# Block attention and a split-precision feed-forward on one core: the weight loads and the split-weight stores issued by GpSimd's queue instead of SP's

## The chip, the core and the metric

The kernel runs on one core of a Trainium2 chip. The metric is the device time of one execution in microseconds; the kernel before has a median of 1163.66 us over 3 runs (1163.17 to 1164.16).

## What is computed

Eight batches of eight heads go through causal block attention (sequence 576, head size 64, blocks of 64), and the result goes through a feed-forward layer with a quadratic gate:

```python
scores = scale * np.matmul(q, k.transpose(0, 1, 3, 2))
mask = block_i >= block_j
scores = np.where(mask, scores, -1000000000.0)
attn = np.exp(scores - np.max(scores, axis=-1, keepdims=True))
attn = attn / (np.sum(attn, axis=-1, keepdims=True) + 1e-09)
x = np.matmul(attn, v)            # -> (4608, 512) after the heads are put side by side
h = x @ w_in                      # (4608, 512) @ (512, 2048)
g = np.where(h >= 1, h, np.where(h <= -1, 0.0, (h + 1) ** 2 / 4))
out = g @ w_out                   # (4608, 2048) @ (2048, 512)
```

q, k and v are float32; the two weight matrices arrive as float64, eight bytes an element.

## The kernel before

**Two parts that overlap.** Attention goes pair of heads by pair of heads (32 pairs, `attention_steps`). The feed-forward goes through 9 chunks of 512 tokens (`c`), and in each through 16 slices of 128 hidden columns (`fc`). `ffn_in` (L852) makes one slice of h in PSUM with three products, high and low halves of x and w_in; ACT and DVE make the gate (L861 to L865), ACT rounds it to its high half `gh` (L866) and GpSimd subtracts it to get the low half `gl` (L867); `ffn_out` multiplies both with the slice of w_out (L880), one step later. The slice of w_out, already split into halves, is read back from the scratch tensor `wo_split` in HBM for each chunk (L869). In the trace the first `gl` starts at 82.10 us.

**The weight pieces.** Before the first chunk can run, the float64 weights must become pairs of float32 words. There are 32 pieces of 128 x 512 (16 of w_in, 16 of w_out), made by `convert` from the generator `weight_pieces`. One piece goes like this:

1. A load brings 512 KB into the tile `bits` (L267). `bits` has three slots, and a load may start when the slot's last reader is done.
2. ACT scales the two halves of the words (L272, L273), DVE clips, shifts and merges them (L274, L277, L280).
3. GpSimd adds the two halves (L286).
4. ACT rounds the sum to the high half (L288: into `wih` or into a staging tile `ws`).
5. GpSimd subtracts to get the low half (L290: into `wil` or `ws`).
6. For a piece of w_out, a store sends the staging tile to `wo_split` (L316). A slot of `ws` can be written again when that store has landed.

In the trace the first load is issued at 0.73 us and the last store at 189.40 us; from there on GpSimd does nothing but `gl`.

**What sets the order.** The order on each engine is written out: the table `QUEUES` holds, for each engine, a list of positions packed as text, and the program ties each instruction to the one in front of it in that order. Each engine works its instructions strictly in that order, so whatever waits holds up all that is listed behind it. DMAs are issued by SP in this kernel (one half of the last output store is issued by ACT). SP's list holds, in the first 190 us, the loads of q, k and v for attention (L433, L440, L444), copies of raw q and k (L387), the masks (L252, L253), the copies of the softmax rows (L348), the reads of `wo_split` (L869), and among them the 32 weight loads and the 16 stores.

**Engines in the text.** PE multiplies and transposes: L494 the first transposes of q and k, L559 the scores of the first batches. ACT's L497 and L499 copy the transposed q and k out of PSUM for L559. DVE's L586 takes row maxima, and L862 and L865 belong to the gate.

Of the kernel before, what the change touches and what calls it, by code (L numbers as in the profile page):

```python
# [11 lines left out]
F32 = mybir.dt.float32  # L12
# [4 lines left out]
I32 = mybir.dt.int32  # L17
# [82 lines left out]
        'avr4!9IO_j+jIP<wb9qip9>eBYQ2yV`U)AJZ{=JOfVBe{F1kw'  # L100
    ),
    "Pool": (
        'c-muNzz-O4@EL)S2~4vBAp|giWf|dWnBZ)LYGfHy)r@eG5lM6ufB*nFCIBn'
    ),
    "SP": (
        'c-rk$yKWOv5IuA6t{=OBc%5K7FR)2W6s1T<LrNMXD5#JS5)}oAf)W~<R1`^>NGWM(kWxe;C11cV<TEHy&YZomAO%=yXmUs6-'
        'JQpoIWt%8AV)Tl0)f(kp^1{(phC|KJJf(SeV_4>)`D8n)0V$Qy-Cd#70|(vaK6%C2%{95M@34PTGC!48sEC~zGuz}pNsV7io'
        '1mYV}Ocz(9<Ie%&3FFYF@D<N}h7|=`qPXqYO6~)y15wo>TYfofM1?sseQ$X>|-s;$Fi7(Y?})5IW-1R7TC(WC_e`QtRI=y+?'
        'Y36v}QT2AQUjv$p}W8@Nw|oLpmyZs4gp@ts7m^xs*$vRV2oieV(gh!;d?<2knZm5EJG&xl`lRP_fLbQK%W({@Z8eU8<nVtvN'
        '=rmlT2OG1Ba{`JU~uqzDT*(c(Rg-|KG(tiDHt9}p1v^tw-d@kxfZ1SzIm`Kj^*w6%lA?;^rIv_*fCl0iyJv){C0p41ReM2}~'  # L110
        'X)_P)mpS4~YtTBfQcQf)-?b&vzM$QiZrMINSx?M^>N>M!L>rp(@8bhqJuxz@D$X&VSV*zJ7kh0BM7&21cQwbDrgdmO*#T$mI'
        'b-S?F#_IMR7_B<Hx4Q;ZQ*B}a%Aob-v_junm_%<AFCI?KXaP!ZLBaKX)70}-dmP#JQ(|@xP2%AZ^Pd*`<LW$W^<BhX^WVm_O'
        'j$EU0*%(n(sB=|I7E{-~L|_0l%LN)17JK>T?cm8a4?'
    ),
}

# [7 lines left out]
def block_attn_then_ffn(  # L124
# [9 lines left out]
    nc = tc.nc  # L134
    B, H, S, D = q.shape
# [43 lines left out]
    def slot(pool, shape, dtype, tag, name):  # L179
        return pool.tile(shape, dtype, tag=tag + next(turns[tag]), name=name)  # L180
# [14 lines left out]
    xl = const.tile([P, NCC, RING], F32R, tag="xl", name="xl")  # L195
# [4 lines left out]
    wo_split = dram.tile([NFC, P, 2, DM], F32, tag="wo_split", name="wo_split")  # L200
# [57 lines left out]
    def wide_tile(dtype, name):  # L258
        return slot(conv, [P, 2 * CW], dtype, "bits", name)

    def convert(n, source, hi, lo, done):

        bits = wide_tile(I32, "bits").rearrange("p (n t) -> p n t", t=2)
        if not shifted:
            shifted.append(att1.tile([P, CW], U32, tag="x32", name="shifted"))
        tmp = shifted[0]
        nc.sync.dma_start(bits, source.bitcast(I32).rearrange("p (n t) -> p n t", t=2))  # L267
        top, low = bits[:, :, 1].bitcast(F32), bits[:, :, 0]
        words = top.bitcast(U32)


        nc.scalar.mul(top, top, 2.0**-112)  # L272
        nc.scalar.mul(low, low.bitcast(U32), 2.0**-29)  # L273
        nc.vector.tensor_scalar(  # L274
            out=top, in0=top, scalar1=F32_TOP, scalar2=-F32_TOP, op0=ALU.min, op1=ALU.max
        )
        nc.vector.tensor_scalar(  # L277
            out=tmp, in0=words, scalar1=3, scalar2=None, op0=ALU.logical_shift_left
        )
        nc.vector.scalar_tensor_tensor(  # L280
            out=words, in0=words, scalar=0x80000000, in1=tmp,
            op0=ALU.bitwise_and, op1=ALU.bitwise_or,
        )
        yield
        w32 = bits[:, :, 1]
        nc.gpsimd.tensor_tensor(out=w32, in0=w32, in1=low, op=ALU.add)  # L286
        w32 = w32.bitcast(F32)
        nc.scalar.copy(hi(), w32)  # L288
        yield
        nc.gpsimd.tensor_tensor(out=lo(), in0=w32, in1=hi().bitcast(F32), op=ALU.subtract)  # L290
        if done:
            done()

    def weight_pieces():

        for f0 in range(0, DF, CW):
            fs = slice(f0, f0 + CW)
            for cc in range(NCC):
                yield (
                    w_in[cc * P : (cc + 1) * P, fs],  # L300
                    lambda cc=cc, fs=fs: wih[:, cc, fs], lambda cc=cc, fs=fs: wil[:, cc, fs], None,
                )
            for fc in range(f0 // P, (f0 + CW) // P):
                ws = {}

                def part(w, d0, ws=ws):
                    if not ws:
                        ws[0] = slot(ffn, [P, 2, DM], F32R, "wo", "ws")
                    return ws[0][:, w, d0 : d0 + CW]

                for d0 in range(0, DM, CW):
                    yield (
                        w_out[fc * P : (fc + 1) * P, d0 : d0 + CW],
                        lambda p_=part, d0=d0: p_(0, d0), lambda p_=part, d0=d0: p_(1, d0),
                        None if d0 + CW < DM else
                        lambda fc=fc, ws=ws: nc.sync.dma_start(wo_split[fc], ws[0].bitcast(F32)),  # L316
                    )

    def prepare_weights():

        live = []
        for n, piece in enumerate(weight_pieces()):
            live = [c for c in live + [convert(n, *piece)] if next(c, True) is None]
            yield
        for _ in range(LAG):
            live = [c for c in live if next(c, True) is None]
            yield
# [662 lines left out]
```

## Time and profile before

| | |
|---|---|
| median of 3 runs | 1163.66 us |
| the profiled execution's own time | 1161.97 us |
| span of the profile in it | 1159.9 us |
| PE busy with matmuls | 1136.7 us (98%) |
| DVE, ACT, GpSimd busy | 700.3, 614.2, 267.7 us |
| weight loads (L267) | 32, 512 KB each |
| stores of split weights (L316) | 16, 512 KB each |

The profile is one execution. "Busy" is time in which an instruction of the engine ran; issuing a DMA is not counted as busy. In rows of the timeline the columns are the start and the duration in us, the engine (SPq is SP's queue issuing a DMA, PEld is PE's weight load), line and operation, output<-input; in square brackets stand the idle time of the engine just before it and what ended that idle time. In rows of groups "x32" is a count.

### The profile page before, as it was taken

The page shows a single profiled execution, that of the slowest core. Times are in us where ns is not written, and L with a number is a line of the kernel's source. Part 1 is how long each engine was busy: PE and PEld are TensorE (multiplying, and loading weights), DVE is VectorE, ACT ScalarE, POOL GpSimd, SP SyncE. Part 2 cuts the span into 40 slices and gives each one's busy share as a digit, 9 for nine tenths or more (in the row PEclk, how much of TensorE's full clock was granted, in tenths as well). Part 3 has the DMA queues.
Part 4 walks back from the last instruction along what each step waited for, and adds up shares of the span by engine and source line. Part 5 has one row for each costly group of instructions (what it writes and reads, how often), then busy time and mean ns, then how long its engine had stood idle before and what let it go on. Part 6 is the DMA issues. An engine that isn't in the chain of part 4 may idle for free.

```text
span 1159.9 us, 19449 instructions
## 1 busy us (share of the span) xinstructions
PE 1136.7 (98%) x6544; PEld 906.6 (78%) x6544; DVE 700.3 (60%) x1731; ACT 614.2 (53%) x1515; POOL 267.7 (23%) x215
## 2 busy tenths in 40 slices
PE   6899999999999999999999999999999999999998
PEld 4667677888887878888888888888888887888886
DVE  7887695766667666666666666666666663222222
ACT  7996675555555555555555555555555553222222
POOL 4445563111111111111111111111111111222222
PEclk9999999999999999999999999999999999999999
DMA  8888787887787866656556555655666443323323
GB/s 227 244 251 264 241 263 228 242 244 221 252 239 245 238 195 181 206 172 188 177 165 214 171 164 176 216 171 167 189 201 177 150 139 110 116 96 105 127 91 108
DMA packets 195793, 219.55 MB, mean 189 GB/s; under 512 B 131296, under 2 KB 145888, under 8 KB 194928
## 3 DMA queue, kind: packets, MB, share of 16 engines
q1 hardware_dynamic: 195552, 218.20, 62.0%
q8 instruction: 52, 0.85, 0.3%
q14 instruction: 45, 0.37, 0.1%
q10 hardware_dynamic: 144, 0.13, 0.0%
HBM read 135.79 MB, written 31.98 MB: 145 GB/s over the span
## 4 chain that ended last, share of the span: by engine, by line
PE 89%; DVE 4%; ACT 2%; DMA 2%; issue 1%; POOL 1%; SPq 0%; POOLq 0%; ACTq 0%
PE ph L852 33%; PE po L880 33%; PE ps_av L730 7%; PE ps_t L651 4%; PE ps_s L535 4%; PE ps_s L536 3%; PE ps_qk L473 1%; PE ps_s L618 1%; ACT pr L591 1%; PE ps_s L559 1%; DMA bits<-in_moe_w_in_dram 1%; DVE nm L586 1%; DVE bits L280 1%; DVE shifted L277 1%; PE ps_s L621 1%
## 5 line engine op out<-in xcount | busy, mean ns | idle before, releaser
L867 POOL TENSOR_TENSOR gl<-t,gh 128x512 fp32r<-128x512 f32 x144 | 188.7, 1311 | 798.3 <-ACT gh L866 720.8
L880 PE MATMUL po<-wo,gh 128*128 128x512 f32 x1152 | 305.6, 397 | 0.2
L880 PEld LDWEIGHTS po<-wo,gh 128*128 128x128 f32 x1152 | 211.5, 188 | 45.4 <-ACT pb L673 0.8
L852 PE MATMUL ph<-xh,wih 128*128 128x512 f32 x576 | 230.4, 400 | 1.1 <-DVE t L865 1.0
L852 PE MATMUL ph<-xl,wih 128*128 128x512 f32 x576 | 226.1, 393 | 0.8 <-DVE xl L743 0.8
L852 PE MATMUL ph<-xh,wil 128*128 128x512 f32 x576 | 225.9, 392 | 0.0
L862 DVE SCALAR_TENSOR_TENSOR t<-t 128x512 f32<-128x512 f32 x144 | 102.6, 713 | 188.9 <-ACT t L861 188.6
L591 ACT ACTIVATE pr<-ps_s,nm 128x384 f32<-128x384 f32 (+3 forms) x256 | 134.2, 529 | 102.1 <-DVE nm L586 85.5
L861 ACT ACTIVATE t<-ph 128x512 f32<-128x512 f32 x144 | 86.2, 599 | 169.5 <-PE ph L852 168.0
L880 PE MATMUL po<-wo,gl 128*128 128x512 f32 x576 | 163.7, 393 | 0.6 <-POOL gl L867 0.6
L866 ACT CAST gh<-t 128x512 fp32r<-128x512 f32 x144 | 89.0, 618 | 105.2 <-DVE t L865 105.1
L586 DVE TENSOR_REDUCE nm<-ps_s 128x1 f32<-128x128 f32 (+3 forms) x256 | 120.8, 484 | 22.7 <-PE ps_s L536 15.4
L880 PEld LDWEIGHTS po<-wo,gl 128*128 128x128 f32 x576 | 108.0, 188 | 25.1 <-POOL gl L867 1.5
L852 PEld LDWEIGHTS ph<-xh,wil 128*128 128x128 f32 x576 | 108.2, 188 | 23.1
L852 PEld LDWEIGHTS ph<-xh,wih 128*128 128x128 f32 x576 | 108.2, 188 | 22.8 <-DVE t L865 2.6
L852 PEld LDWEIGHTS ph<-xl,wih 128*128 128x128 f32 x576 | 108.3, 188 | 20.0 <-DVE xl L743 1.1
L865 DVE TENSOR_TENSOR t<-ph,t 128x512 f32<-128x512 f32 x144 | 98.7, 686 | 2.2
L651 PEld LDWEIGHTS ps_t<-ident_r,prr 128*128 128x128 f32 x600 | 68.3, 139 | 23.5 <-issue 2.4
L673 ACT COPY pb<-ps_t 128x512 f32<-128x512 f32 (+1 forms) x128 | 68.2, 534 | 13.1 <-PE ps_t L651 12.1
L598 DVE TENSOR_SCALAR pr<-pr,sm 128x128 f32<-128x128 f32 (+2 forms) x192 | 70.6, 389 | 4.3
L651 PE MATMUL ps_t<-ident_r,prr 128*128 128x128 f32 x600 | 71.3, 236 | 1.2 <-ACT t L861 0.7
L541 DVE TENSOR_SCALAR sm<-sm 128x1 f32<-128x1 f32 x192 | 28.7, 153 | 71.6 <-ACT pr L591 69.9
(108 smaller groups left out, 1401.7 us busy)
## 6 DMA issues: line engine op xcount, KB each, us to landing
wo<-wo_split SPq DMA_DIRECT2D x144, 512.0 KB, 3.6
prr<-pr SPq DMA_DIRECT2D x96, 192.0 KB, 3.0
prr<-pr SPq DMA_DIRECT2D x48, 256.0 KB, 2.4
out_dram<-ob SPq DMA_DIRECT2D x35, 256.0 KB, 3.4
bits<-in_moe_w_in_dram SPq DMA_DIRECT2D x16, 512.0 KB, 4.9
vs<-in_v_dram SPq DMA_DIRECT2D x64, 128.0 KB, 3.3
bits<-in_moe_w_out_dram SPq DMA_DIRECT2D x16, 512.0 KB, 4.0
wo_split<-ws SPq DMA_DIRECT2D x16, 512.0 KB, 4.3
```

Of the source, the lines that this page charges most:

```text
L586: nc.vector.tensor_reduce(out=nm[:, i : i + 1], in_=ps[:, cs], axis=AX.X, op=ALU.max, negate=True)
L591: nc.scalar.activation(raw[:, cs], ps[:, cs], AF.Exp, bias=nm[:, i : i + 1], scale=1.0, accum_out=sm[:, i : i + 1],)
L598: nc.vector.tensor_scalar_mul(pr[:, cs], raw[:, cs], sm[:, i : i + 1])
L651: nc.tensor.transpose(out.bitcast(F32R), src, ident_r)
L730: nc.tensor.matmul(ps[j * D : (j + 1) * D, lo_col:], self.vs[j][:, kt, :], x, start=i == 0, stop=i == len(heads[0]) - 1,)
L852: nc.tensor.matmul(ph, w[:, cc, fs], x[:, cc, xs], start=(cc == 0 and i == 0), stop=(cc == NCC - 1 and i == 2),)
L861: nc.scalar.activation(t_, ph, AF.Relu, bias=0.5, scale=0.5)
L862: nc.vector.scalar_tensor_tensor(out=t_, in0=t_, scalar=1.0, in1=t_, op0=ALU.min, op1=ALU.mult)
L865: nc.vector.tensor_tensor(out=t_, in0=ph, in1=t_, op=ALU.max)
L866: nc.scalar.copy(gh, t_)
L867: nc.gpsimd.tensor_tensor(out=gl, in0=t_, in1=gh.bitcast(F32), op=ALU.subtract)
L880: nc.tensor.matmul(po[tt], g[:, ts_], wo[:, w, :], start=(fc == 0 and g is gh and w == 0), stop=fc == NFC - 1 and g is gl,)
```

## The change

Two calls are made on GpSimd's queue instead of SP's, and the tables of GpSimd and SP are written anew to fit. The lists of PE, DVE and ACT are the same as before, and on SP and GpSimd what stays keeps its order.

```diff
     "Pool": (
-        'c-muNzz-O4@EL)S2~4vBAp|giWf|dWnBZ)LYGfHy)r@eG5lM6ufB*nFCIBn'
...
-        nc.sync.dma_start(bits, source.bitcast(I32).rearrange("p (n t) -> p n t", t=2))
+        nc.gpsimd.dma_start(bits, source.bitcast(I32).rearrange("p (n t) -> p n t", t=2))
         top, low = bits[:, :, 1].bitcast(F32), bits[:, :, 0]
...
                         None if d0 + CW < DM else
-                        lambda fc=fc, ws=ws: nc.sync.dma_start(wo_split[fc], ws[0].bitcast(F32)),
+                        lambda fc=fc, ws=ws: nc.gpsimd.dma_start(wo_split[fc], ws[0].bitcast(F32)),
```

On SP, at the start of the program, before:

```order
L985 UNCONDITIONAL_BRANCH
L267 DMA bits<-in_moe_w_in_dram 128x1024
L440 DMA qn<-in_q_dram 128x4x64 x2
L444 DMA en<-in_q_dram 64x2x64
L440 DMA kn<-in_k_dram 128x4x64 x2
L444 DMA en<-in_k_dram 64x2x64
L267 DMA bits<-in_moe_w_in_dram 128x1024
L252 DMA qa<-mrow 4x512
L253 DMA ka<-mrow 4x512
L267 DMA bits<-in_moe_w_in_dram 128x1024
```

and now:

```order
L985 UNCONDITIONAL_BRANCH
L440 DMA qn<-in_q_dram 128x4x64 x2
L444 DMA en<-in_q_dram 64x2x64
L440 DMA kn<-in_k_dram 128x4x64 x2
L444 DMA en<-in_k_dram 64x2x64
L252 DMA qa<-mrow 4x512
L253 DMA ka<-mrow 4x512 x2
```

The loads of q (L440) are now SP's first, and the three weight loads are gone from between them. On GpSimd the first weight load stands behind the memset of the identity (`masks.py:197`), and the second and third behind the two selects that build the identity and the mask rows.

On GpSimd, where the last pieces of w_in and the first of the last pieces of w_out are made (the trace of before has this at 151.8 to 165.4 us; the numbers behind `bits`, `gl`, `t` and `gh` tell the buffers apart), before:

```order
L290 TENSOR_TENSOR wil_97<-bits_1896,wih_96 128x512
L286 TENSOR_TENSOR bits_1934<-bits_1934 128x512
L867 TENSOR_TENSOR gl_1918<-t_1916,gh_1917 128x512
L290 TENSOR_TENSOR wil_97<-bits_1934,wih_96 128x512
L286 TENSOR_TENSOR bits_1988<-bits_1988 128x512
L867 TENSOR_TENSOR gl_2010<-t_2008,gh_2009 128x512
L290 TENSOR_TENSOR wil_97<-bits_1988,wih_96 128x512
L286 TENSOR_TENSOR bits_2026<-bits_2026 128x512
```

and now:

```order
L290 TENSOR_TENSOR wil_97<-bits_1896,wih_96 128x512
L267 DMA bits_1988<-in_moe_w_in_dram 128x1024
L267 DMA bits_2026<-in_moe_w_out_dram 128x1024
L286 TENSOR_TENSOR bits_1934<-bits_1934 128x512
L867 TENSOR_TENSOR gl_1918<-t_1916,gh_1917 128x512
L290 TENSOR_TENSOR wil_97<-bits_1934,wih_96 128x512
L267 DMA bits_2078<-in_moe_w_out_dram 128x1024
L286 TENSOR_TENSOR bits_1988<-bits_1988 128x512
L867 TENSOR_TENSOR gl_2010<-t_2008,gh_2009 128x512
L290 TENSOR_TENSOR wil_97<-bits_1988,wih_96 128x512
L267 DMA bits_2119<-in_moe_w_out_dram 128x1024
L286 TENSOR_TENSOR bits_2026<-bits_2026 128x512
```

Four loads now stand in GpSimd's list between its adds and subtractions. The load into `bits_1988` was SP's before, free to go when the subtraction in front of the one shown first was done; now it stands behind both.

On GpSimd, at the last pieces of all (173 to 185 us in the trace of before), before:

```order
L290 TENSOR_TENSOR ws_2117<-bits_2078,ws_2117 128x512
L290 TENSOR_TENSOR ws_2146<-bits_2119,ws_2146 128x512
L286 TENSOR_TENSOR bits_2148<-bits_2148 128x512
L290 TENSOR_TENSOR ws_2223<-bits_2148,ws_2223 128x512
L867 TENSOR_TENSOR gl_2170<-t_2168,gh_2169 128x512
```

and now:

```order
L290 TENSOR_TENSOR ws_2117<-bits_2078,ws_2117 128x512
L316 DMA wo_split_100<-ws_2117 128x1024
L290 TENSOR_TENSOR ws_2146<-bits_2119,ws_2146 128x512
L316 DMA wo_split_100<-ws_2146 128x1024
L286 TENSOR_TENSOR bits_2148<-bits_2148 128x512
L290 TENSOR_TENSOR ws_2223<-bits_2148,ws_2223 128x512
L867 TENSOR_TENSOR gl_2170<-t_2168,gh_2169 128x512
L316 DMA wo_split_100<-ws_2223 128x1024
```

Two stores stand ahead of the add of the last piece, and the last store behind a `gl`.

More of the change, by code (lines that the diff above doesn't have):

```diff
@@ L102 @@
     "Pool": (
-        'c-muNzz-O4@EL)S2~4vBAp|giWf|dWnBZ)LYGfHy)r@eG5lM6ufB*nFCIBn'
+        'c-rkwQ5JwO2m)uT`=2<6X1%&Xe8`5t6EG|gL;Rh|TfLK4#v@}fO&Z(D>PwZF^6knn_z0feHRN~gys}HR$3L4)omSnK({&BCP'
+        'xYO<8&Mar)gOryC`|ys'
     ),
     "SP": (
[L106 to L113, printed above, removed]
+        'c-rk!yKYlK5IwVd?{%(iVLK4pNgS|&1R)BlR7sfz2?{DCgp>kNfG8-TphhW386<vy4~Rrcz97Gl&q#?lb9QqDDH1CUO?I^Ra'
+        'c1VsoY^f=G!|%v7CPJ&H~1{@S{}nk>=J1UtrbzB%vpQ%e<AALlv^RnY9b5tI{uPh2YfFRFXauy2e^T>+UV*T$XaTrxX(mQ)}'
+        'yb_42Ut+X^Y3%kXfy<TdH8JkknM{pyGdEWQ)6O>X<Yp-adChUf0*fh&d%Tsboo&JhH-b_2yHH>ert=ys;kr1Datbwuo2Etf_'
+        'sQe}(!h>6!8Gj#M9W9*c?%80J}*>SK{SXBE?0$4_+&BCBG5YX0}cR`FFF9X|KSvo3~#vIm;JuWi*I;*hATdBOLJPVf=GMv93'
+        'Tb8ZhcFJMaiM7Z<yxKHs-r?hWJ!ng3=7T7n$^H_6_*s<T{jJsA5omodp0yX`jzt7!Oc85%^ujb8I!Go+ksIDuUAllSi{|KMx'
+        '8cLDjp5mPInS~q+{IIvSOvVjrxT`tFJgx8MlO5~s1x_d6J~;wDSZr?M1n-<wT59nZoN{FD8o$Rxj?CX<Mjxsdzc)8E;oDeaK'
+        'JuxYt#ochzQ17XzvlQ<2Hu8?GDqj^d}gc3w0w$~qxM90m9DRzd9C+a@Bh^sGVf&(0e`Oo^R0Q~()t5%`7;&'
     ),
```

## The prediction

> **What bounds the kernel now.** I read the page first, then a table of stretches, then the waits of PE, then the timeline where PE or ACT waits. The page:
>
> ```profile
> span 1159.9 us, 19449 instructions
> PE 1136.7 (98%) x6544; PEld 906.6 (78%) x6544; DVE 700.3 (60%) x1731; ACT 614.2 (53%) x1515; POOL 267.7 (23%) x215
> PE 89%; DVE 4%; ACT 2%; DMA 2%; issue 1%; POOL 1%; SPq 0%; POOLq 0%; ACTq 0%
> ```
>
> PE is busy for all but 23.2 us, so the end moves only by what PE idles more or less. The stretches (from:to, length, then busy time of PE, PEld, DVE, ACT, POOL; clock, DMA share, GB/s) show where it idles:
>
> ```profile
> 6.10:20.00 13.90, 11.31 (x78) 7.07 (x78) 11.18 (x29) 10.83 (x29) 5.73 (x5) 1.00 0.83 230
> 20.00:80.00 60.00, 54.60 (x530) 37.68 (x530) 52.50 (x129) 55.82 (x152) 27.50 (x23) 1.00 0.85 246
> 80.00:150.00 70.00, 68.08 (x436) 48.49 (x436) 51.81 (x102) 48.17 (x108) 35.31 (x30) 1.00 0.81 255
> 150.00:170.00 20.00, 19.37 (x111) 15.07 (x111) 18.51 (x27) 15.22 (x31) 15.66 (x12) 1.00 0.85 271
> 170.00:190.00 20.00, 19.08 (x135) 13.98 (x134) 12.75 (x27) 9.18 (x25) 8.54 (x7) 1.00 0.72 218
> 190.00:1159.90 969.90, 964.21 (x5260) 784.35 (x5259) 550.37 (x1409) 472.68 (x1172) 173.74 (x133) 1.00 0.59 178
> ```
>
> After 190 us nothing of the change is left, and the work there is fixed. Everything is decided in the first 190 us, where PE idles 6.1 us ahead of its first transpose and 2.6 + 5.4 + 1.9 + 0.6 + 0.9 = 11.4 us behind it. From 20 to 80 us ACT is the fullest engine (55.8 of 60 us); from 80 us on PE is (68.1 of 70). GpSimd is fullest from 150 to 170 us, 15.7 of 20 us.
>
> PE's waits name a DMA in one place that matters, before the first transpose:
>
> ```profile
> PE ps_qk L494 <- DMA qn<-in_q_dram: 6.2, 1, 6.2
> ```
>
> So PE is hardly held by DMAs, and SP's queue, relieved of 48 issues, gives little back after the start.
>
> **The price X of one issue on GpSimd.** The trace has no DMA on GpSimd. The rows of this work, by tile (durations min/median/max in ns):
>
> ```profile
> L274 DVE TENSOR_SCALAR bits<-bits x32: 407/427/1081, 6.3 to 179.0; 128x512 f32<-128x512 f32 x32
> L277 DVE TENSOR_SCALAR shifted<-bits x32: 410/428/1414, 6.7 to 179.5; 128x512 uint32<-128x512 uint32 x32
> L280 DVE SCALAR_TENSOR_TENSOR bits<-bits,shifted x32: 680/693/1843, 7.2 to 179.9; 128x512 uint32<-128x512 uint32 x32
> L286 POOL TENSOR_TENSOR bits<-bits x32: 1034/1040/1487, 8.0 to 180.7; 128x512 int32<-128x512 int32 x32
> L290 POOL TENSOR_TENSOR ws<-bits,ws x16: 1292/1307/1779, 28.6 to 183.0; 128x512 fp32r<-128x512 f32 x16
> DMA to landing us min/median/max: 3.4/4.6/6.1
> ```
>
> Nearest rows: below, an issue on SP (0.33 us, in the timeline rows further down); above, GpSimd's slowest operation here, 1.78 us. I take X = 1.04 us, the median of GpSimd's cheapest pass over 128 partitions (L286), because the issue is work on GpSimd over 128 rows and not on SP. The Trainium skill, DMA: Bandwidth & Descriptors, section Latency and other measured facts, says that a first byte takes about 1 us on the software path against 0.6 us on the hardware one; an estimate of X from that page is 1 us, and the sum would be the same.
>
> Forty-eight issues at 1.04 us are 50 us more on an engine that is busy 94 us of the first 190 (the five rows above with the 1.2 us of the first 6.1 us: page of before, 267.7 - 173.7). On average that fits; from 150 to 170 us it doesn't: five issues are 5.2 us, and 15.66 + 5.2 is over 20.
>
> **Part 1, the start.**
>
> ```profile
> 0.73 0.39 SPq L267 DMA_DIRECT2D bits<-in_moe_w_in_dram  x1
> 1.18 1.33 SPq L440 DMA_DIRECT2D qn<-in_q_dram  x2
> 5.05 0.65 ACT L273 ACTIVATE bits<-bits 128x512 int32<-128x512 uint32 x1 [3.02 <-DMA bits<-in_moe_w_in_dram]
> 6.16 1.09 PE L494 MATMUL ps_qk<-ident_r,qn 128*128 128x128 f32 x4 [6.16 <-DMA qn<-in_q_dram]
> 7.29 0.60 ACT L497 ACTIVATE qk<-ps_qk 128x512 f32<-128x512 f32 x1 [1.04 <-PE ps_qk L494]
> 13.02 0.68 ACT L272 ACTIVATE bits<-bits 128x512 f32<-128x512 f32 x1 [0.76 <-DMA bits<-in_moe_w_in_dram]
> ```
>
> With the weight load out of its front, SP issues q at 0.73 instead of 1.18 us: PE starts 0.45 us earlier, at 5.7. But ACT's list has the first piece ahead of L497. GpSimd can issue it after its memset, at about 0.93 us, done at 1.97 instead of SP's 1.12: ACT's two passes begin at 5.9 and L497 at 7.1, so of the 0.45 only 0.2 us is left. The third load, on SP stuck behind other loads, goes out on GpSimd by about 6 us, and ACT's wait of 0.76 us goes with it. Together -1.0 us. Bounds: -2 us if q's 256 KB also land a microsecond sooner without 512 KB in front of them (the nearest row: 3.4 us shortest against 4.6 us median to landing), +0.5 us if X is 1.78.
>
> **Part 2, 150 to 170 us.**
>
> ```profile
> 150.46 2.80 POOL L290 TENSOR_TENSOR wil<-bits,wih 128x512 fp32r<-128x512 f32 x2 [0.64 <-ACT wih L288]
> 151.83 0.34 SPq L267 DMA_DIRECT2D bits<-in_moe_w_in_dram  x1
> 153.29 0.34 SPq L267 DMA_DIRECT2D bits<-in_moe_w_out_dram  x1
> 153.94 1.37 POOL L286 TENSOR_TENSOR bits<-bits 128x512 int32<-128x512 int32 x1 [0.68 <-PE po L880]
> 157.06 0.68 ACT L272 ACTIVATE bits<-bits 128x512 f32<-128x512 f32 x1 [0.68 <-DMA bits<-in_moe_w_in_dram]
> 157.85 0.33 SPq L267 DMA_DIRECT2D bits<-in_moe_w_out_dram  x1
> 159.58 1.24 POOL L286 TENSOR_TENSOR bits<-bits 128x512 int32<-128x512 int32 x1 [1.75 <-DVE bits L280]
> 163.93 1.49 POOL L286 TENSOR_TENSOR bits<-bits 128x512 int32<-128x512 int32 x1
> 164.00 0.33 SPq L267 DMA_DIRECT2D bits<-in_moe_w_out_dram  x1
> 165.45 0.65 ACT L288 CAST ws<-bits 128x512 fp32r<-128x512 f32 x1 [1.61 <-POOL bits L286]
> 167.66 0.33 PE L559 MATMUL ps_s<-qk 64*64 64x64 f32 x3 [0.57 <-ACT qk L497]
> ```
>
> This is a chain in which everybody already waits: ACT for a load (157.06), GpSimd for DVE (159.58), ACT for GpSimd (165.45), PE for ACT (167.66). The load that ACT waits for was issued by 152.17; on GpSimd it stands behind the second subtraction, which ends at 153.26, and is done at 153.26 + 1.04 = 154.30, 2.13 us later. The add of 159.58 comes 2.1 us later by that. A further load (SP's at 157.85) lies in the gap behind GpSimd's subtraction; SP's at 164.00 now stands ahead of the add of 163.93, which had no idle time before it: another 1.04 us. ACT's L288 and with it PE come 2.13 + 1.04 = 3.2 us later. If the loads, no longer in line behind SP's other transfers, land in 3.4 instead of 4.6 us, it is 2.0. I take the middle, +2.6 us. By the bounds of X it is 1.1 + 2 x 0.33 = 1.8 and 1.1 + 2 x 1.78 = 4.7 us, or 0.6 for the small X with early landing.
>
> **Part 3, 177 to 186 us.**
>
> ```profile
> 177.37 0.33 SPq L316 DMA_DIRECT2D wo_split<-ws  x1
> 182.28 0.66 ACT L288 CAST ws<-bits 128x512 fp32r<-128x512 f32 x1 [0.82 <-DMA wo_split<-ws]
> 185.62 0.73 PE L880 MATMUL po<-wo,gl 128*128 128x512 f32 x2 [0.37 <-POOL gl L867]
> ```
>
> ACT waits for this store to free its staging slot, GpSimd then for ACT, PE for GpSimd's `gl`. The store ends its issue at 177.70 on SP; on GpSimd it starts at 177.5 (the store ahead of it has pushed the subtraction by 0.2) and ends at 178.5: +0.8 us, all of it on PE. Bounds +0.1 and +1.6.
>
> **Part 4, DVE beside GpSimd.** The maxima of DVE's three rows are two to three times their medians. The means of the same groups in the first 190 us:
>
> ```profile
> L280 DVE SCALAR_TENSOR_TENSOR bits<-bits,shifted 128x512 uint32<-128x512 uint32 x32 | 28.5, 890 | 0.8
> L277 DVE TENSOR_SCALAR shifted<-bits 128x512 uint32<-128x512 uint32 x32 | 17.7, 552 | 0.8
> L274 DVE TENSOR_SCALAR bits<-bits 128x512 f32<-128x512 f32 x32 | 16.3, 514 | 6.1 <-ACT bits L272 1.8 <-POOL bits L286 1.5 <-POOL wil L290 1.4
> ```
>
> Above their medians that is 32 x (197 + 124 + 87) ns = 13 us, beside 94 us of GpSimd work: 0.14 us for each. If issues hold DVE as GpSimd's arithmetic seems to, 50 us more make 7 us of DVE time. DVE has 4% of the chain, 46 us, of the 190: a quarter, so 1.7 us would count; at the other end nothing, if an issue doesn't hold DVE. I take +0.9. Elsewhere (20 to 150 us) GpSimd is idle for more than half of the time, and I take 0, with up to +2 as an upper bound.
>
> **Sum.** -1.0 + 2.6 + 0.8 + 0.9 = +3.3 us. The profiled execution took 1161.97 us (its span 1159.9 and 2.1 around it), 1.7 below the median of the runs; on it the sum gives 1165.3, on the median of 1163.66 it gives **1167.0 us**.
>
> **The rivals.**
>
> *No measurable change.* X is small, or its queueing fits in GpSimd's idle time, and the start's gain pays the rest: with X near 0.5 us, parts 2 and 3 are 1.1 and 0.3 (early landings), part 4 about 0.2, the start -1.2: +0.4, 1164.1 us. For it speaks that GpSimd idles half of the time; against it, that the dense stretch is just where others wait for it. The Trainium skill, DMA: Bandwidth & Descriptors, section Issuing engines are not separate DMA queues, says that issuing from several engines saves only the issue time, usually small; by that rule this rival is the outcome, and the one DMA wait of PE above agrees.
>
> *Faster.* The loads leave a queue in which they stood behind others. It needs an X of 0.33 us, as on SP, and landings near 3.4 us: start -2, the wait of 0.68 us at 157.06 gone, part 2 then 0.6 - 0.7, part 3 +0.1, and part of ACT's time from 20 to 80 us used better, -1. About -3 us, 1160.7. X decides: above some 0.5 us it is lost in part 2.
>
> *Much slower.* Issues are stretched by DVE as DVE is by GpSimd, to X = 2.5 us: part 2 is 1.1 + 5.0 = 6.1, part 3 2.3, part 4 1.7, the start +1, and between 20 and 150 us some +3: +14, 1177.8 us. The long DVE rows show that the two hold each other up. The Trainium skill, SBUF — State Buffer, section SBUF: two separate sides, says that GpSimd can't write descriptors while DVE runs in its two-port mode; that is this rival, and no run here shows it yet.
>
> **Chances.** Forecast 0.52, no change 0.22, faster 0.13, much slower 0.13. About 0.2% (2.3 us) is what a measurement of this kernel can tell from no change. The forecast's own range reaches into the band of no change, which takes a little from it: faster 0.13, same 0.27, slower 0.60. The range from 1161.0 to 1175.0 goes from just above the faster case to the forecast with X at 1.78 (+0.5 + 4.7 + 1.6 + 1.7 = +8.5, with the +2 between and early or late landings up to 11), and leaves out most of the first and the last rival.
>
> **What would show it.** Right: GpSimd's issue rows near 1 us; ACT's L288 near 165 us waiting 3 us longer for L286, PE's L559 behind it; PE's idle time in the first 190 us up from 17.6 to some 21 us; nothing changed after. Part 1 shows in the first transpose at 5.7 and L497 near 7.1 us. The forecast is wrong if issue rows are under 0.5 us (then faster or same), if DVE's L274 and L277 means jump (then much slower), or if loads land so early that no ACT wait on them is left.

## The result, and the profile after

| | before | after |
|---|---|---|
| median | 1163.75 us (4 runs, 1163.17 to 1164.16) | 1180.18 us (4 runs, 1176.26 to 1183.49) |
| ratio | | 1.0142, 95% interval 1.0122 to 1.0162 |
| profiled execution, span | 1161.97, 1159.9 us | 1177.81, 1176.0 us |

The change costs 16.4 us, over the upper end of the range. From the page of after:

```profile
span 1176.0 us, 19451 instructions
PE 1140.9 (97%) x6544; PEld 907.4 (77%) x6544; DVE 706.0 (60%) x1731; ACT 614.3 (52%) x1515; POOL 293.2 (25%) x263
PE 80%; DMA 6%; DVE 6%; ACT 4%; issue 2%; POOL 1%; SPq 1%; POOLq 0%; DVEq 0%; ACTq 0%
bits<-in_moe_w_in_dram POOLq DMA_DIRECT2D x16, 512.0 KB, 5.8
bits<-in_moe_w_out_dram POOLq DMA_DIRECT2D x16, 512.0 KB, 5.0
wo_split<-ws POOLq DMA_DIRECT2D x16, 512.0 KB, 5.1
```

PE has 4 us more work by its records and 12 us more idle time; DMA's share of the chain that ends last went from 2% to 6%. GpSimd's own issues are in its busy time here, other than the section on the profile before says: x263 is 215 instructions and 48 issues. The last three rows give the median time from issue to landing; the page of before has 4.9, 4.0 and 4.3 us there. The stretches of after, in the columns shown for before:

```profile
6.10:20.00 13.90, 10.20 (x71) 6.42 (x72) 9.60 (x23) 9.30 (x24) 5.21 (x5) 1.00 0.80 231
20.00:80.00 60.00, 52.24 (x508) 35.94 (x506) 51.24 (x126) 54.20 (x147) 35.92 (x40) 1.00 0.79 229
80.00:150.00 70.00, 64.30 (x405) 45.69 (x399) 50.73 (x96) 46.21 (x104) 42.21 (x44) 1.00 0.77 235
150.00:170.00 20.00, 17.72 (x101) 11.57 (x101) 14.73 (x24) 12.49 (x27) 12.05 (x13) 0.91 0.77 244
```

Most PE time is lost from 20 to 150 us, where the forecast had none, and GpSimd still idles there for some 40% of the time, issues counted as busy. Set against each other by the start of the same GpSimd instruction, after lags before by 2.5 us at 9.8 us (of before's time), 3.1 at 26, 4.5 at 45, 5.5 at 82, 7.0 at 121, 9.4 at 134, 11.1 at 155, 13.1 at 164, 13.3 at 191, 13.4 at 202, and 16.1 at the end. The granted clock fell to half for 3.4 us near 164 us, up to 1.7 us of it.

Who waits: ACT's waits for DMAs in the first 210 us, before and after (sum, times, longest):

```profile
ACT bits L273 <- DMA bits<-in_moe_w_in_dram: 3.0, 1, 3.0
ACT bits L272 <- DMA bits<-in_moe_w_in_dram: 2.1, 3, 0.8
ACT ws L288 <- DMA wo_split<-ws: 0.8, 1, 0.8
ACT bits L272 <- DMA bits<-in_moe_w_out_dram: 0.6, 1, 0.6
```

```profile
ACT ws L288 <- DMA wo_split<-ws: 7.1, 5, 3.5
ACT bits L273 <- DMA bits<-in_moe_w_in_dram: 5.4, 1, 5.4
ACT bits L272 <- DMA bits<-in_moe_w_in_dram: 4.0, 5, 1.4
ACT bits L272 <- DMA bits<-in_moe_w_out_dram: 2.9, 5, 1.0
```

6.5 us before, 19.4 after: 12.9 us more, about as much as the lag at 191 us (13.3). That points at these waits, but a sum of waits isn't yet a loss: the experiments below take some of them away. One such place, first in after, then in before (timeline rows of GpSimd, SP and ACT):

```profile
36.56 1.29 POOL L290 TENSOR_TENSOR ws<-bits,ws 128x512 fp32r<-128x512 f32 x1 [0.78 <-ACT ws L288]
38.26 0.61 POOL L267 DMA_DIRECT2D bits<-in_moe_w_in_dram  x1 [0.41 <-POOL ws L290]
44.80 0.65 ACT L272 ACTIVATE bits<-bits 128x512 f32<-128x512 f32 x1 [1.38 <-DMA bits<-in_moe_w_in_dram]
49.22 1.29 POOL L290 TENSOR_TENSOR ws<-bits,ws 128x512 fp32r<-128x512 f32 x1 [3.36 <-ACT ws L288]
```

```profile
34.82 0.35 SPq L267 DMA_DIRECT2D bits<-in_moe_w_in_dram  x1
40.25 0.70 ACT L272 ACTIVATE bits<-bits 128x512 f32<-128x512 f32 x1
```

The slot comes free when the subtraction ends, at 37.85 us. GpSimd waits 0.41 us for its own result before it issues, the issue takes 0.61, and the data are there 6.95 us after the slot was free; in before ACT starts 5.43 us after the issue and waits for nothing. The add, the rounding and the next subtraction follow late.

### The profile page after: what moved, and what is told of

It is laid out like the page before. It is cut to its first block, busy times and chain, and to the rows that moved or that the text cites. A ratio compares the mean times of both kernels' runs of the same rounds, so it can differ in the third digit from the quotient of the medians.

```text
span 1176.0 us, 19451 instructions
## 1 busy us (share of the span) xinstructions
PE 1140.9 (97%) x6544; PEld 907.4 (77%) x6544; DVE 706.0 (60%) x1731; ACT 614.3 (52%) x1515; POOL 293.2 (25%) x263
## 4 chain that ended last, share of the span: by engine, by line
PE 80%; DMA 6%; DVE 6%; ACT 4%; issue 2%; POOL 1%; SPq 1%; POOLq 0%; DVEq 0%; ACTq 0%
PE po L880 30%; PE ph L852 30%; PE ps_av L730 6%; PE ps_t L651 4%; PE ps_s L535 3%; PE ps_s L536 2%; DMA wo_split<-ws 2%; ACT pr L591 1%; PE ps_qk L473 1%; PE ps_s L618 1%; DMA kc<-kb 1%; DMA prr<-pr 1%; DVE bits L280 1%; DVE bits L274 1%; DMA en<-in_k_dram 1%
## 5 line engine op out<-in xcount | busy, mean ns | idle before, releaser
L673 ACT COPY pb<-ps_t 128x512 f32<-128x512 f32 (+1 forms) x128 | 68.3, 534 | 13.7 <-PE ps_t L651 12.6
```

## The experiments

Theories after the traces: **T1**, transfers leave and land later, and ACT waits for them; **T2**, the 48 issues take up GpSimd's list; **T3**, at the start the second and third load compete with the first q and k. In each kernel the lists of the other engines stay as they are; a moved DMA takes the place that before or the change gives it. Lines of these kernels stand 7 to 30 lower; the text uses before's.

All runs, each beside before on the same chip. "Equal clock": half-clock stretches differ from run to run, so to set parts side by side I fitted all 218 runs with a level for each chip, a difference for each kernel and one slope on the clock loss (1 - granted clock, times the span); the slope came out at 0.74 us per us (0.61 to 0.86). Of the change's partner runs only one has a clock on record, 1.0, which I used for all four. The ± are 95%. Some kernels have the dips in all their runs (e2: a clock of 0.992 to 0.994 in all four), and in the kept traces they stand directly behind waits of PE (last section); so the plain difference is the price of a version, and the fit only shares it out.

Against the expectations printed below: e7, e10, e13, e17, e18 and e19 came out in a range that one theory gave, e1 in that of T2, which e5 and e9 then spoke against. e4, e5, e9 and e15 fell between the ranges of the two theories, e14 and e16 less than 1 us above their upper ends, and e2, e3, e8, e11 and e12 outside all of them (e3 below, the others above).

| run | what is on GpSimd | us, before | ratio, interval | difference | at equal clock |
|---|---|---|---|---|---|
| the change | 32 loads, 16 stores | 1180.2, 1163.8 | 1.0142 (1.0122, 1.0162) | +16.4 | +12.8 ± 2.1 |
| e1 | 32 loads | 1175.7, 1161.9 | 1.0127 (1.0110, 1.0144) | +13.9 | +11.8 ± 1.8 |
| e2 | 16 stores | 1174.7, 1161.9 | 1.0116 (1.0100, 1.0133) | +12.8 | +8.3 ± 2.0 |
| e3 | loads 4 to 32, stores | 1170.9, 1161.9 | 1.0074 (1.0059, 1.0089) | +9.1 | +8.6 ± 1.8 |
| e4 | 48 memsets | 1169.0, 1161.9 | 1.0061 (1.0046, 1.0076) | +7.2 | +7.6 ± 1.8 |
| e5 | 48 small DMAs | 1166.5, 1163.7 | 1.0028 (1.0016, 1.0039) | +2.8 | +2.7 ± 1.3 |
| e7 | loads 1 to 3 | 1165.4, 1163.7 | 1.0021 (1.0009, 1.0033) | +1.7 | +2.5 ± 1.1 |
| e8 | loads 4 to 32 | 1175.6, 1163.7 | 1.0104 (1.0090, 1.0118) | +11.9 | +9.0 ± 1.6 |
| e9 | 29 small DMAs (loads' places) | 1164.9, 1163.7 | 1.0018 (1.0005, 1.0031) | +1.2 | +1.8 ± 1.0 |
| e10 | 16 small DMAs (stores' places) | 1165.0, 1162.7 | 1.0023 (1.0010, 1.0035) | +2.2 | +1.9 ± 1.1 |
| e11 | nothing; small DMAs ahead on SP | 1177.1, 1162.7 | 1.0121 (1.0101, 1.0140) | +14.4 | +10.6 ± 1.6 |
| e12 | nothing; small DMAs behind on SP | 1174.8, 1162.7 | 1.0100 (1.0082, 1.0119) | +12.1 | +7.9 ± 1.5 |
| e13 | e8 with a 4th bits slot | 1174.2, 1162.5 | 1.0098 (1.0079, 1.0118) | +11.7 | +7.9 ± 1.5 |
| e14 | nothing; 4th bits slot | 1164.7, 1162.5 | 1.0012 (0.9998, 1.0026) | +2.2 | +1.1 ± 1.1 |
| e15 | the change, 4th bits slot | 1174.7, 1162.5 | 1.0104 (1.0079, 1.0130) | +12.2 | +11.6 ± 1.3 |
| e16 | e3 with a 4th bits slot | 1173.3, 1162.5 | 1.0084 (1.0062, 1.0106) | +10.9 | +7.5 ± 1.4 |
| e17 | e2 with a 3rd ws slot | 1165.8, 1163.7 | 1.0021 (1.0009, 1.0033) | +2.1 | +1.7 ± 1.1 |
| e18 | nothing; 3rd ws slot | 1163.3, 1163.7 | 0.9999 (0.9987, 1.0011) | -0.4 | -0.2 ± 1.0 |
| e19 | e3 with a 3rd ws slot | 1173.0, 1163.7 | 1.0078 (1.0065, 1.0091) | +9.3 | +8.2 ± 1.4 |

### GpSimd's own time: e4, e5, e9, e10

```diff
-        nc.gpsimd.dma_start(bits, source...)       # the change
+        nc.sync.dma_start(bits, source...)         # on SP, at before's place
+        nc.gpsimd.memset(filler, 0.0)              # e4, 128 x 640 bf16
+        nc.gpsimd.dma_start(filler[:, 2*k : 2*k+2], w_in[:P, k : k+1]...)   # e5, e9, e10: 8 bytes x 128
```

> All DMAs go from SP as before; at each of the 48 places that the change gives them in GpSimd's list stands a memset of a spare tile, estimated to take about 0.6 us, as long as the DMA instructions did there. T1 (what costs is where and when the transfers are issued and land): 1163 to 1166 us. T2 (what costs is GpSimd's time): 1172 to 1180. The bits waits stay at before's 3.0 and 2.1 us under T1.

> All DMAs of the kernel go from SP as before; at each of the 48 places that the change gives them in GpSimd's list stands a DMA of one word of 8 bytes for each of 128 partitions into a spare tile: the same kind of instruction, with 48 KB moved in all instead of 25 MB. T2 (GpSimd's time, 0.58 us a piece, is what costs): like the memsets, 1167 to 1171 us, some 7 over before, of it some from 30 us on, at the adds (bits) that ScalarE's and GpSimd's next steps wait for. T1 (what costs is the late landing): 1162 to 1164, since the real transfers are issued and land as before.

> All DMAs of the kernel go from SP; at the places of the loads 4 to 32 in GpSimd's list stands a DMA of 8 bytes a partition into a spare tile. T2: 29 of 48 instructions, 1165.5 to 1168 us, and the same as the run with the real loads there. T1: 1162 to 1163.

> All DMAs of the kernel go from SP; at the 16 places of the stores in GpSimd's list stands a DMA of 8 bytes a partition into a spare tile. T2 (GpSimd's time): all of what the run with the real stores there lost beside its dips of the clock, about 6 us, so 1168 to 1170 where before takes 1163. T1 (what costs is that the store leaves and lands later, and ScalarE's rounding copy waits for the ws slot): 1163 to 1165.5 us.

The groups of the small DMAs in e5, and of the change's own:

```profile
L275 POOL DMA_DIRECT2D filler<-in_moe_w_in_dram x48 | 26.9, 561 | 0.4 <-issue 0.4
```

```profile
L316 POOL DMA_DIRECT2D wo_split<-ws x16 | 9.3, 581 | 2.0 <-POOL ws L290 2.0
L267 POOL DMA_DIRECT2D bits<-in_moe_w_out_dram x16 | 9.2, 575 | 3.0 <-POOL wil L290 1.1 <-DVE sums L637 0.7 <-POOL ws L290 0.4
L267 POOL DMA_DIRECT2D bits<-in_moe_w_in_dram x16 | 9.2, 573 | 2.3 <-POOL ws L290 1.2 <-POOL wil L290 0.7 <-issue 0.4
```

561 ns against 573 to 581: the small DMAs fill the list like the real ones, and cost 2.8 us. That is T2, and it falls as the main cause. One thing the small DMAs lack: they wait for nothing (0.4 us of idle time ahead of them), while GpSimd idles 2.0 + 3.0 + 2.3 = 7.3 us ahead of the real issues. So e5, e9 and e10 price the issues, and not what waits in GpSimd's list cost beside them. The memsets looked like support for it (+7.2 for 639 ns each), but they did something that the DMAs don't. DVE's rows in e4:

```profile
L305 DVE TENSOR_SCALAR shifted<-bits 128x512 uint32<-128x512 uint32 x32 | 22.4, 698 | 0.8
L302 DVE TENSOR_SCALAR bits<-bits 128x512 f32<-128x512 f32 x32 | 20.5, 644 | 3.2 <-issue 1.6 <-POOL wil L318 1.4 <-ACT bits L300 0.2
```

698 and 644 ns, against 552 and 514 in before and 573 and 527 in e5: GpSimd's memsets stretch DVE, its DMA issues hardly do. A stand-in must be of the same kind as what it stands for.

### The start: e7, e3

```diff
+        (nc.gpsimd if n < 3 else nc.sync).dma_start(bits, ...)   # e7, stores on SP
+        (nc.sync if n < 3 else nc.gpsimd).dma_start(bits, ...)   # e3, stores on GpSimd
```

> Only the first three loads go from GpSimd, at the change's places; the other 29 and all stores go from SP as before. T3 (the second and third load, out at 3.9 us on a ring of their own, compete with the first q and k loads): the first transpose starts 1.0 to 1.7 us later than before's 6.2 us, the first adds 2 to 3 us later, and the run takes 1164 to 1167 us, 2 to 5 over before. If the loss at the start is caught up where PE waits less later, it ends within 1 us of before.

> The first three loads go from SP at their old places, all other loads and all stores from GpSimd. T3: the first transpose starts near 6.2 us again, and the 2.5 to 3 us that the change lost in its first 20 us come back: 1173 to 1178 us, 2 to 4 us under the change. T1 and T2: the rest of the loss stays, above all the waits of the rounding copy for the stores (16 us or so of ws waits in the first 210 us).

The start in after (SP, GpSimd, ACT, PE), then PE in e7:

```profile
0.74 1.34 SPq L440 DMA_DIRECT2D qn<-in_q_dram  x2
1.32 0.70 POOL L267 DMA_DIRECT2D bits<-in_moe_w_in_dram  x1 [0.37 <-issue]
3.94 1.12 POOL L267 DMA_DIRECT2D bits<-in_moe_w_in_dram  x2
7.41 0.66 ACT L273 ACTIVATE bits<-bits 128x512 int32<-128x512 uint32 x1 [5.39 <-DMA bits<-in_moe_w_in_dram]
7.89 1.09 PE L494 MATMUL ps_qk<-ident_r,qn 128*128 128x128 f32 x4 [7.89 <-DMA qn<-in_q_dram]
10.04 1.08 PE L494 MATMUL ps_qk<-ident_r,kn 128*128 128x128 f32 x4 [1.06 <-DMA kn<-in_k_dram]
```

```profile
7.05 1.09 PE L510 MATMUL ps_qk<-ident_r,qn 128*128 128x128 f32 x4 [7.05 <-DMA qn<-in_q_dram]
10.73 1.09 PE L510 MATMUL ps_qk<-ident_r,kn 128*128 128x128 f32 x4 [2.58 <-DMA kn<-in_k_dram]
```

q is issued 0.44 us earlier than in before and lands 1.7 later. What the DMA engines moved from 3.0 to 4.5 us (packets, MB, share of the engines' time), first in after, then in before; q0 is GpSimd's queue, q1 is SP's:

```profile
q0 software_dynamic: 76, 0.31, 92.8%
q1 hardware_dynamic: 17, 0.00, 1.2%
```

```profile
q1 hardware_dynamic: 775, 0.41, 93.3%
```

SP has issued both loads of q by 2.08 us, but for 1.5 us its queue moves next to nothing, and the first weight load, alone on GpSimd's queue, has the engines. (e7 is the same: 85 packets against 5.) So it is the first load that makes q late. T3 named the second and third: these are issued from 3.94 us on, where SP had them at 5.23 and 7.45, behind q and k, and what they hold up is k and what follows (from 6.5 to 10.5 us GpSimd's queue moves 0.99 of 1.18 MB). e7 has the three loads alone: its lag is 2.2 us by 45 us and still 2.2 at 265; its profiled execution then loses 2.2 more, for which no cause is shown. In e3 the first transpose is at 6.03 us again. So T3 holds for the three loads together, at 2 to 3 us; no run moves them one by one.

### The stores: e2, e17, e18

```diff
-                        ws[0] = slot(ffn, [P, 2, DM], F32R, "wo", "ws")
+                        ws[0] = slot(...) if fc % 2 == 0 else next(turns["wo"]) and more   # e17, e18
+    more = const.tile([P, 2, DM], F32R, tag="kb", name="ws")   # where kb lies later
```

> The stores go from GpSimd as in the change, the loads from SP as before. T1: it keeps the waits of the rounding copy (ws) for the store, 6 us: 1168 to 1171 us. T2: 16 of 48 instructions remain, a third of 16: 1168 to 1170. T3: nothing of the loss at the start remains, the first transpose starts near 6.2 us as before. Waits of ScalarE for the landing of bits fall back to 3.0 and 2.1 us.

> Stores from GpSimd, loads from SP, as in the run that took 1174.7 us; every second ws lies where kb lies later, so that no two neighbouring ws share a slot. If the waits of the rounding copy for the store are the cause: they fall from 14 us to under 4 and the time to 1163 to 1167 us, near the run with small DMAs at the stores' places (1165). If the store's ring beside SP's is the cause: the waits go and the time stays, 1171 to 1176.

> The control: the kernel before with the same third slot for ws, all DMAs on SP. Before waited 0.8 us for a store's slot, so 1160 to 1164 us, within 1 us of before.

ACT's waits for stores in e2, and one of them (GpSimd, ACT); then the same store in before (GpSimd, SP):

```profile
ACT ws L304 <- DMA wo_split<-ws: 13.9, 6, 4.2
```

```profile
143.53 1.28 POOL L306 TENSOR_TENSOR ws<-bits,ws 128x512 fp32r<-128x512 f32 x1 [6.61 <-ACT ws L304]
145.99 0.57 POOL L271 DMA_DIRECT2D wo_split<-ws  x1
151.23 0.66 ACT L304 CAST ws<-bits 128x512 fp32r<-128x512 f32 x1 [4.23 <-DMA wo_split<-ws]
```

```profile
134.26 1.30 POOL L290 TENSOR_TENSOR ws<-bits,ws 128x512 fp32r<-128x512 f32 x1 [3.90 <-ACT ws L288]
135.59 0.32 SPq L316 DMA_DIRECT2D wo_split<-ws  x1
```

On SP the store starts 0.03 us after the subtraction has ended (134.26 + 1.30); on GpSimd 1.2 us after, behind a `gl`, and ACT gets the slot 6.4 us after the subtraction, 4.23 of which it stands idle. PE feels such waits through ACT: behind an earlier one of 3.12 us, PE waits 2.97 us for ACT's `pr` and goes on at 144.82. With a third slot, ACT waits for no store in e17; the waits for DMAs that are left are the loads':

```profile
ACT bits L295 <- DMA bits<-in_moe_w_in_dram: 3.1, 4, 1.2
ACT bits L296 <- DMA bits<-in_moe_w_in_dram: 2.8, 1, 2.8
ACT bits L295 <- DMA bits<-in_moe_w_out_dram: 0.4, 1, 0.4
```

and the loss falls from 12.8 to 2.1 us, that of the small DMAs at the same places (e10, 2.2). The half clock goes with the waits: the mean clock loss is 8.2 us in e2 and 1.9 in e17. The slot alone changes nothing (e18). So what stores on GpSimd cost, beyond the issues, is the wait for the staging slot. This part is shown.

### The loads: e1, e8, e11 to e14

```diff
+        (nc.sync if n < 3 else nc.gpsimd).dma_start(bits, ...)     # e8; e1 without the condition
+        nc.sync.dma_start(bits[:, 3:], ...)                        # e11, e12: from the 4th load on, and
+        for c in range(3): nc.sync.dma_start(bits[:, c : c+1], ...)   # 3 small ones ahead (e11), behind (e12)
+        bits = bits3 if n % 4 == 3 else conv.tile(..., tag=f"bits{n % 4}")   # e13, e14: bits3 where kb lies later,
+        # and from the 5th on each load stands where the one ahead of it stood (two excepted)
```

> The loads of the weight pieces go from GpSimd as in the change; the stores of the split output weights go from SP as before. T1 (pieces land later, and the stores hold the ws slots longer): of the 13 us that the change has lost by 204 us, some 6.6 belong to waits of ScalarE for loads and 6.3 to waits for stores, so this one keeps the first: 1170 to 1174 us. T2 (the time that the DMA instructions take in GpSimd's own list delays its adds): 32 of the 48 instructions remain, two thirds of 16: 1173 to 1176. T3 (the second and third load compete with the first q and k loads): the first transpose starts near 7.9 us as in the change.

> The first three loads and all stores go from SP, the loads 4 to 32 from GpSimd. T3: 3 us under the run with all loads on GpSimd, near 1169 to 1171 with the dips of the clock left out. T1 and T2 can be told apart only beside the run with small DMAs at these 29 places: T2 gives the same time for both, T1 puts this one 3 us or more above.

> Everything on SP as before; from the fourth load on, three of the 512 columns go as three small DMAs ahead of the rest of the load, so that the rest is issued about 1 us after its slot came free, as it is from GpSimd (0.33 us a piece on SP), while GpSimd's list is that of before. T1: the time is that of the run with the real loads 4 to 32 on GpSimd without its dips, 1168 to 1173 us, and 4 us or more above the run with the same small DMAs behind the rest. T2: 1163 to 1166, equal to that run.

> The control of the run with the small DMAs ahead: the same three small DMAs stand behind the rest of each load, so SP issues the same instructions and all that stands behind them on SP is as late, but the bulk of the load leaves as early as before. Both theories: 1163 to 1167 us; what it takes over before is the price of 87 more issues on SP and of the last small piece landing behind the rest.

> Loads 4 to 32 from GpSimd, the first three and all stores from SP, as in the run that took 1175.6 us; but the pieces turn through four slots instead of three (the fourth lies where kb lies later), and each load from the fifth on stands one place of the list earlier. Lateness (T1): the 1 us by which a load is late is hidden by about 5 us of slack, what stays is GpSimd's own time, 1164 to 1167 us. Shared engines: the loads still run beside SP's transfers, 1171 to 1176.

> The kernel before with the fourth slot, all DMAs on SP, each load from the fifth on one place earlier. Both theories: before's own waits for loads after the first are under 3 us in all, so 1160 to 1164 us; it also shows whether earlier loads cost the q, k and v loads behind them anything.

Loads 4 to 32 cost 11.9 us (9.0 at equal clock), small DMAs at their places 1.2 (1.8). T1 is right against T2 as far as the issues themselves go (GpSimd idles 5.8 us ahead of e8's issues and not at all ahead of e9's; what that costs no run separates), but lateness alone doesn't carry it. e11 and e12 make loads late with nothing on GpSimd and lose 14.4 and 12.1, but the control lost nearly as much as the run: ACT's L272 waits 12.6 us for loads in e12 too (2.7 in before), since its small pieces land last and SP is late for everything. The pair doesn't separate the causes. In e13 the fourth slot takes ACT's waits for loads below before's (3.9 us, against 5.7), and yet the time stays:

```profile
ACT bits L302 <- DMA bits<-in_moe_w_in_dram: 2.9, 1, 2.9
ACT bits L301 <- DMA bits<-in_moe_w_in_dram: 1.0, 1, 1.0
```

Two things are seen in its place. One is order. e13, then before:

```profile
77.69 0.57 POOL L294 DMA_DIRECT2D bits<-in_moe_w_in_dram  x1 [0.41 <-POOL ws L319]
77.75 0.49 SPq L377 DMA_DIRECT2D xl<-pr  x1
85.24 0.69 ACT L620 ACTIVATE pr<-ps_s,nm 128x512 f32<-128x512 f32 x1 [2.14 <-DMA xl<-pr]
85.29 0.51 PE L680 MATMUL ps_t<-ident_r,xl 128*128 128x128 f32 x4 [1.75 <-DMA xl<-pr]
```

```profile
73.33 0.49 SPq L348 DMA_DIRECT2D xl<-pr  x1
73.86 0.67 SPq L267 DMA_DIRECT2D bits<-in_moe_w_out_dram  x1
```

On SP the copy of softmax rows went ahead of the load. Now the load is issued 0.06 us ahead of it on another queue, the copy is there after 7.4 us, and PE and ACT wait (in e8 too: 1.9 and 2.3 us); in before nobody waits for it. The Trainium skill, DMA: Bandwidth & Descriptors, section Queues, rings and completion order, says that a DMA engine takes turns between the queues that have work for it, packet by packet. e13 agrees in that both queues move data at once (from 80 to 82.5 us 120 packets and 0.46 MB of GpSimd's, 205 and 0.18 MB of SP's); the start of after, with 76 packets against 17, shows that the turns needn't be even. The other is the clock:

```profile
82.80:86.20 3.40, 1.38 (x7) 0.83 (x8) 0.73 (x2) 1.26 (x4) 1.87 (x2) 1.00 0.63 148
86.20:93.00 6.80, 6.80 (x20) 3.91 (x20) 5.42 (x13) 3.22 (x8) 1.70 (x2) 0.50 0.72 243
```

The half clock follows directly on the wait for `xl`, with PE busy for 1.38 of 3.40 us. The same stands at 21.3 us: 10.2 us at half clock behind 3.40 in which PE was busy for 0.85. In all e13 ran 17 us at half clock. So, as far as these rows go, the clock isn't a cause beside the waits but follows on some of them. At equal clock the slot gains 1.1 us over e8, and 2.2 if its own price on SP (e14, +1.1) is taken off.

### Both cures in the change: e15, e16, e19

> The whole change with the fourth slot. Lateness: the loss of the loads goes, the start (1.7 to 3 us) and the waits of the rounding copy (ws) for the stores (5 to 7 us) stay: 1168 to 1174, 6 us or more below the change. Shared engines: within 4 us of the change, 1176 to 1181.

> As the whole change with the fourth slot, but the first three loads from SP. Lateness: only the stores' part and GpSimd's own time stay, 1166 to 1170 us, 2 to 4 below the whole change with the slot. Shared engines: within 2 us of the run without the slot, 1169 to 1173.

> The change with the first three loads from SP and the third slot for ws. If start and ws waits are the two largest parts: 1166 to 1170 us; what is left over before is GpSimd's own time (3) and the loads that land later (2 to 4). If lateness and ws waits are only where the loss shows and not its cause, it stays where the run without the slot was, 1170 to 1173.

At equal clock the fourth slot gains 1.2 us in the change (12.8 to 11.6) and 1.1 in e3 (8.6 to 7.5), each within its uncertainty. The third slot of ws, which cured the stores alone, does next to nothing beside late loads (8.6 to 8.2, within the uncertainty): ACT's waits for stores are gone from e19's list, and its waits for loads grew from e3's 9.2 us to 11.3. It looks as if late loads and late stores held the same chain, one behind the other: loads alone cost 9.0, stores alone 8.3, both 8.6.

## Why the prediction was wrong

- **X was no failure.** 0.57 to 0.58 us an issue, inside 0.33 to 1.78 and better than the 1.04 taken; with 0.41 us of waiting for GpSimd's own result it is 1.0. e5 puts the price of 48 issues at 2.8 us. That this is close to the +3.3 of the whole sum is luck: the forecast had it from 150 to 186 us and on DVE, while e5's profiled execution has lost its 4 us by 107 us and loses nothing more up to 190.
- **Part 1 had the wrong sign.** "The third load, on SP stuck behind other loads, goes out on GpSimd by about 6 us" was counted as a gain, and so was q ahead of the first load. But on its own queue the first load overtook q at the DMA engines (76 packets against 17 from 3.0 to 4.5 us), and the third went out at 3.94 us, with the second, beside k. q's issue came as forecast (0.74 for 0.73), the first transpose at 7.89 for 5.7, L497 at 9.01 for 7.1: -1.0 forecast, 2 to 3 us lost (e7).
- **"Elsewhere (20 to 150 us) GpSimd is idle for more than half of the time, and I take 0"** is the step that failed most. The lag grows by 8.6 us there (2.5 to 11.1). A moved DMA was priced by its issue, and GpSimd's idle time was to cover that. For the stores what counted in its place was the time until a `ws` slot was free again: 16 of them cost 12.8 us, and 2.1 with a third slot (e2, e17). For the loads it was more than the time from a free slot to landed data: with a fourth slot ACT waits less for them than in before, and the loss stays (e13). What they held up on SP's queue is seen in the `xl` rows; how much of the loss that is stays open.
- **"Land in 3.4 instead of 4.6 us"** was an expectation without a row. The medians rose, 4.9 to 5.8, 4.0 to 5.0 and 4.3 to 5.1 us.
- **Part 2 came near in size by luck.** The lag grows by 1.6 us from 151.8 to 167.5 us of before's time (+2.6 forecast), but the half clock can be all of that, and the chain of the forecast didn't come: the L288 that was to wait 3 us longer waits 1.81 us, against 1.61, and PE's wait of 0.57 us for L497 is gone.
- **Part 3 was about right.** The lag grows by 0.4 us from 176.0 to 184.3 (+0.8 forecast); ACT waits 1.41 us for the store, against 0.82, and PE 0.63 us for `gl`, against 0.37.
- **Part 4**: DVE's L277 and L274 have means of 547 and 558 ns, against 552 and 514; 32 x (44 - 5) ns = 1.2 us of DVE time, of 7 feared. By the prediction's own quarter 0.3 us of that would count, where the sum took 0.9.
- **"After 190 us nothing of the change is left"**: 2.7 us more are lost after 202 us, part of it where PE waits for SP's copies (0.9 us for `kc`, 0.5 for `qa`). Why SP's copies are later there I didn't test.
- **The rivals.** "Much slower" named 1177.8 us, near the result, but by DVE starving the issues, and they took 0.58 us. "No change" rested on the rule that it cites from the Trainium skill, DMA: Bandwidth & Descriptors, section Issuing engines are not separate DMA queues, that another issuing engine saves only issue time; e5 shows that the issue time is indeed small. The same section of the Trainium skill says that all DMAs run on the same 16 engines and interleave; the first 11 us of after show what that can cost.

**The account** at equal clock, as far as the parts add up: 12.8 us, of which GpSimd's own time 2.7 (e5) and the start 2.5 (e7); the 7 to 8 left are late loads and stores and transfers that lost their order. For the stores the slot wait is shown. For the loads, slack recovers 1 to 2 us; that the rest is lost order is argued from the `xl` rows and not shown in size, and waits in GpSimd's list may have a part in it. The other 3.6 us of 16.4 go with the half clock: the change's four runs lost 4.7 us of clock on average, and at 0.74 that is 3.5. It belongs to the price of the change as far as the half clock follows on waits of PE, as the last section has it.

None of these versions beats before; the best (e18) equals it.

## What to carry to other kernels

A DMA queue is also an order of priority: before moving transfers off it, list what they stood behind and what is then issued beside them. Where tiles turn through two or three slots, price the time from a free slot to landed data, and see who waits in order for it; idle time of the issuing engine says nothing on that. To tell issue time from transfer time, put small DMAs in the same places; and don't add up causes that hold the same chain.

## What the runs showed of the hardware

- An issue on GpSimd over 128 partitions takes 0.56 us for 1 KB and 0.58 us for 512 KB; behind its own arithmetic it first waits 0.3 to 0.4 us.
- Memsets of 639 ns on GpSimd stretch DVE's 514 and 552 ns passes to 644 and 698; DMA issues of 561 ns only to 527 and 573.
- Two 128 KB loads of q issued on SP by 2.08 us and a 512 KB load issued on GpSimd at 1.32 us did not share the DMA engines evenly: from 3.0 to 4.5 us GpSimd's queue moved 0.31 MB and SP's 17 packets.
- Half-clock stretches of 3.4 us and multiples of it came with most of the kernels that lost much (mean loss 4 to 8 us in e1, e2, e8 and e11 to e13), though hardly in e3 or e4 (1.2 and 0.6). In the kept traces there are 23 ahead of the end, and each starts directly behind 3.4 us in which PE was busy for 19% to 74% (in after, at 162.0, for 2.52 of 3.40 us). But not each such stretch is followed by one: e9 had 1.75 of 3.40 us busy from 17.8 us on and kept its clock. The Trainium skill, TensorE: Matmul & The Clock Gate, Part 1, ties the half rate to idle windows of about 3.4 us; the length agrees, but PE was not idle throughout any of these, and how idle is enough the runs don't show.
